# Retention and low-rank mixer on one core: load order of batch 1, place of batch 3's last loads, and first tiles of MLP1

## The chip, the cores and the metric

The kernel runs on one core of a Trainium2 chip. The metric is the device time of one execution in microseconds (us), given as the median of several runs. Engines are named as in the profile: PE (TensorE matmuls) with PEld (its weight loads), DVE (VectorE), ACT (ScalarE), POOL (GpSimd), SP (SyncE, which here issues nearly all DMAs; a row marked SPq is such an issue).

## What is computed

For each of 4 batches there are 768 tokens, 8 heads of 64 columns and a model width of 512. A retention layer gives x, and a mixer with a two-layer MLP follows:

```python
for t in range(S):                       # per head, gamma = 1 - 2^(-5-h)
    state = gamma * state + k[t] v[t]^T
    y[t] = q[t] @ state / sqrt(64)
x = y                                    # (4, 768, 512)
u = x + V^T (U^T x)                      # over tokens: U is 768x32, V is 32x768
out = u + relu(u @ w_ch1) @ w_ch2        # 512 -> 2048 -> 512
```

Inputs and output are fp32; the matmuls run in bf16.

## The kernel before

**Tiling.** A batch has six chunks of 128 tokens (c = 0 to 5). Retention is done chunk by chunk: kd and qd are k and q times powers of gamma (`ret_k`, `ret_q`, lines 251 and 256, both on POOL), vb is v cast to bf16 (`ret_v`, line 262, ACT). Kd and qd are transposed into qkT, for batch 1 on PE (`ret_T`, line 419, eight 128x128 transposes for a chunk) and for batches 2 and 3 by DMA (`ret_T_dma`, line 282, two DMA transposes on SP for a chunk). `ret_S` makes the masked scores a (line 441, DVE), `ret_O` the output x of a chunk (line 460, ACT). There are four buffers for qd and six for kd, and six for each of the loaded tiles k_n, q_n and v_n.

**The mixer.** `mix_P` makes P = U^T x. `mix_n` (lines 527 to 535) makes u for one chunk of tokens, j, adds x on DVE (line 531), casts it on ACT (line 533) and has it transposed into uT by a DMA on SP (line 535). Batches 2 and 3 do so for all six chunks, batch 1 for chunks 3 to 5; its chunks 0 to 2, the first half of uT, are made by PE in four pieces, one for each of the four 128-row blocks of the model width (`mix_u`), and evicted by ACT or DVE (`evict`, lines 120 and 124).

**The MLP.** `mlp1(b, m, hf)` is one tile: four matmuls of 384 columns (c = 0 to 3, the four blocks of uT) that sum into one PSUM bank, evicted with a relu into gT. There are 16 values of m and two halves hf of the tokens, 32 tiles in all, 128 matmuls. `mlp2` then takes, for each chunk of tokens, 16 matmuls of 512 columns, a DVE addition (line 576) and the DMA of the result (line 579).

**What sets the order.** The program is written out by hand, and every engine works in the order of the program. For each batch b the list of main slots (32 of MLP1, then 48 or more of MLP2) is woven with side work of batch b + 1: `put(side, i, f)` places f ahead of main slot i. While batch b runs its MLP, the retention and the mixer of batch b + 1 are done between its slots. All loads and DMA transposes share SP's queue, which issues in order. In the table of batch b = 0, all loads of batch 1 are placed at slot 14 (line 701), chunk by chunk as k, q, v (`load_chunk`, line 138; `load_one`, line 131; the issue itself is line 135). The first three loads are gated by a small ACT write (line 134), so that they do not start before slot 14. Loads of batch 3 stand in the table of b = 1, in `ret_side` at slots 31, 36, 41, 46, 68 and 72 (line 617), the u transposes of batch 2 at slots 62 to 67.

**MLP1's order.** For b of 1 and more, line 707 puts the first six tiles of the first half of the tokens first, then the six of the second half, and then alternates. Two DMA-transposed halves are so needed at different times. In batch 0 the first tiles go through `mlp1_two`, which takes two tiles at a time: blocks 0 and 1 of both, and then blocks 2 and 3 of both.

Of the kernel before, what the change touches and what calls it, by code (L numbers as in the profile page):

```python
# [47 lines left out]
def kernel(  # L48
# [14 lines left out]
    NCK = S // P  # L63
# [36 lines left out]
    def set_banks(main, mix=None):  # L100

        for who, banks in (("main", main), ("mix", mix)):
            use[who] = banks and sorted(banks, key=lambda i: taken.get(i, 0))
            n_use[who] = 0

    def mm_bank(who="main"):
        if use[who] is None:
            who = "main"
        b = use[who][n_use[who] % len(use[who])]
        n_use[who] += 1  # L110
        taken[b] = n_bank[0]
        return bank(b)

    def matmul(o, l, r, cols, **kw):
        nc.tensor.matmul(o, l, r, **kw)  # L115
        bal.mm(cols)

    def evict(o, i, cols, relu=False, dve_rate=1.0):
        if bal.pick(cols, dve_rate) == "A":
            nc.scalar.activation(o, i, AF.Relu if relu else AF.Copy)  # L120
        elif relu:
            nc.vector.tensor_relu(o, i)
        else:
            nc.vector.tensor_copy(out=o, in_=i)  # L124


    staged = {}
# [3 lines left out]
    def load_one(t, b, c, src, nm):  # L131
        n = rin.tile([P, H, D], fp32, tag=nm, name=f"{nm}_{b}_{c}")
        if (b, c) == gate:
            nc.scalar.activation(n[:, 0, :1], lsc, AF.Copy)
        nc.sync.dma_start(out=n, in_=src[b, :, ts(c, P), :].rearrange("h p d -> p h d"))  # L135
        t[nm, c] = n

    def load_chunk(b, c):
        t = {}
        for src, nm in ((k, "k_n"), (q, "q_n"), (v, "v_n")):  # L140
            load_one(t, b, c, src, nm)
        staged[b, c] = (t["q_n", c], t["k_n", c], t["v_n", c])

    NG = P // RK
    Vs = wts.tile([RK, S], bf16)
# [5 lines left out]
    def load_w1(lo, w):  # L151
        nc.gpsimd.dma_start(
            out=w1b[:, :, ds(lo, w)],
            in_=moe_w_ch1[:, ds(lo, w)].rearrange("(c p) m -> p c m", p=P))

    def load_w2(s):
        nc.gpsimd.dma_start(
            out=w2b[:, ds(4 * s, 4)],
            in_=moe_w_ch2[ts(s, 512)].rearrange("(j p) c -> p j c", p=P))
# [9 lines left out]
    for what in ("q0", "kA", "q1", "k2", "k3", "vA", "q2", "k4", "v2", "k5", "v3", "v4", "v5"):  # L169
        src, i = {"q": q, "k": k, "v": v}[what[0]], what[1]  # L170
# [75 lines left out]
    st_p = {}  # L246

    def ret_k(b, c, eng):
        q_n, k_n, v_n = staged.pop((b, c))
        kd = rmid.tile([P, H, D], bf16, tag="kd", name=f"kd_{b}_{c}", bufs=6)  # L250
        eng.tensor_tensor(kd, k_n, Gk[:, c].unsqueeze(2).to_broadcast([P, H, D]), op=ALU.mult)  # L251
        rc[b, c] = dict(kd=kd, q_n=q_n, v_n=v_n)
# [7 lines left out]
    def ret_v(b, c):  # L260
        vb = rmid.tile([P, H, D], bf16, tag="vb", name=f"vb_{b}_{c}", bufs=6)
        nc.scalar.activation(vb, rc[b, c]["v_n"], AF.Copy)  # L262
        bal.book("A", 0.63)
        rc[b, c]["vb"] = vb
# [4 lines left out]
    def ret_in(b, c):  # L269
        ret_k(b, c, nc.gpsimd)  # L270
        ret_q(b, c, nc.gpsimd)
        if b == 1 and c in EARLY:
            load_chunk(b + 1, c - EARLY[0])

    def by_dma(b):
        return b >= 2
# [148 lines left out]
    def ret_S(b, cs):  # L425

        for c, bks in zip(cs, ((SA, SB), (OB, TP if by_dma(b) else 2))):
            r = rc[b, c]
            r["s"] = [bank(i) for i in bks]
            for p in range(NP):  # L430
                for e in (0, 1):
                    matmul(r["s"][e][:, ts(p, P)], r["kT"][ds(D * e, D), p],
                           r["qT"][ds(D * e, D), p], 80, start=True, stop=True)
        for c in cs:
            rc[b, c]["a"] = rmid.tile([P, 2, NP, P], bf16, tag="a", name=f"a_{b}_{c}", bufs=5)
            for e in (0, 1):
                ret_mask(b, c, e)
# [109 lines left out]
    def mlp1_two(b, ms, hf):  # L547
        if b not in gTs:
            gTs[b] = gtp.tile([P, NM, S], bf16, tag="gT", name=f"gT_{b}")
        g = [mm_bank()[:, :HS] for _ in ms]  # L550
        for cs in ((0, 1), (2, 3)):
            for m, o in zip(ms, g):
                for c in cs:
                    matmul(o, w1b[:, c, ts(m, P)], uTs[b][:, c, ts(hf, HS)], HS, start=(c == 0),
                           stop=(c == NCB - 1))
        for m, o in zip(ms, g):
            evict(gTs[b][:, m, ts(hf, HS)], o, HS, relu=True)
# [23 lines left out]
    def mlp1_slots(b, first=0):  # L581
        return [lambda m=m, hf=hf: mlp1(b, m, hf) for m in range(first, NM) for hf in (0, 1)]

    def mlp2_slots(b, of=8):

        cols = {(B - 1, NCK - 1): ((0, DM // 2), (DM // 2, DM // 4), (3 * DM // 4, DM // 4))}
        return [lambda j=j, i=i: mlp2(b, j, i, 12 if (b, j) in cols else of,
                                      cols.get((b, j), ((0, DM),)))
                for j in range(NCK) for i in range(12 if (b, j) in cols else of)]

    def weave(main, side):

        for i, f in enumerate(main):
            for g in side.pop(i, []):
                g()
            f()
        for i in sorted(side):
            for g in side[i]:
                g()

    def put(side, i, f):
        side.setdefault(int(i), []).append(f)

    def ret_side(b, at, lead, S_at, O_at, side):


        for c in range(NCK):
            put(side, max(0, at[c] - lead), lambda c=c: ret_in(b, c))
            put(side, O_at[c] - 3, lambda c=c: ret_v(b, c))
        for cs in S_at:  # L610
            put(side, S_at[cs], lambda cs=cs: ret_S(b, cs))
        for f, when in ((ret_T, at), (ret_O, O_at)):
            for c in range(NCK):
                put(side, when[c], lambda c=c, f=f: f(b, c))
        if by_dma(b) and b + 1 < B:
            for c in range(NCK):
                put(side, (31, 36, 41, 46, 68, 72)[c], lambda c=c: load_chunk(b + 1, c))
        return side

    def mix_side(b, i, side):  # L620
        put(side, i + 2, lambda: mix_P(b))
        js = [j for j in range(NCK) if by_token(b, j)]
        for n, j in enumerate(js):
            put(side, i + 5 + n, lambda j=j: mix_n(b, j))
        if b == 1:
            for c in range(NCB):
                put(side, i + 5 + len(js) + c, lambda c=c: mix_u(b, 0, c))
        return side
# [56 lines left out]
    for b in range(B):  # L685
        nxt = b + 1 < B
        slots = mlp1_slots(b)
        n1 = len(slots)
        side = {}
        set_banks([0, 1, 2, SA, SB, OB])  # L690
        if b == 0:
            taken.update({i: n for n, i in enumerate((1, 2, 0, OB, SA, SB, TP))})
            set_banks([1, 2, 0, OB, SA, SB, TP])
            slots[:4] = [lambda: mlp1_two(0, (0, 1), 0), lambda: None,
                         lambda: mlp1_two(0, (0, 1), 1), lambda: None]
            for i, s in ((1, 2), (2, 3)):
                put(side, i, lambda s=s: load_w1(512 * s, 512))
            for s in range(4):
                put(side, 4 + s, lambda s=s: load_w2(s))
            for c in range(NCK):  # L700
                put(side, 14, lambda c=c: load_chunk(1, c))
            at, lead, mix_at = [n1 + 7 + 5 * c for c in range(NCK)], 4, n1 + 38
            S_at = {(0, 1): n1 + 14, (2, 3): n1 + 24, (4,): n1 + 30, (5,): n1 + 35}
            O_at = [n1 + i for i in (19, 22, 29, 32, 35, 38)]
        if b:

            slots = slots[:12:2] + slots[1:12:2] + slots[12:]
        if b and nxt:
            set_banks([0, 1, 2])
            at, lead, mix_at = [10 + 4 * c for c in range(NCK)], 5, n1 + 25  # L710
            S_at = {(0, 1): 27, (2, 3): 37, (4, 5): 47}
            O_at = [32, 35, 43, 46, 53, 56]
        if nxt:
            ret_side(b + 1, at, lead, S_at, O_at, side)
            put(side, n1, lambda: set_banks([0, 1], [2]))
            put(side, mix_at, lambda: use.update(mix=[2, SA, SB]))
            mix_side(b + 1, mix_at, side)
        if b == 1:
            for c, i in ((3, 0), (4, 7), (5, 15)):
                put(side, i, lambda c=c: load_chunk(2, c))  # L720
        weave(slots + mlp2_slots(b), side)


# [28 lines left out]
```

## Time and profile before

| what | value |
|---|---|
| median of 3 runs | 228.08 us (227.82 to 229.71) |
| the profiled execution | 228.57 us, of which the span of the profile is 226.80 us |
| granted TensorE clock | 1.00 |
| DMA over the span | 34.85 MB, mean 154 GB/s |
| start of MLP1 of batch 0, 1, 2, 3 | 27.43, 81.88, 131.92, 181.95 us from the span's start |

Rows of the profile give the start in us from the span's start, the length, the engine, the line of the kernel, the operation, output and inputs, and the number of merged instructions. In square brackets stands how long the engine sat idle ahead of the row, and what ended that. A matmul's end is modelled, so waits of PE are better read from the distance of two starts. In views of waits the numbers are the total in us, the count and the longest.

### The profile page before, as it was taken

To read this page: it belongs to the slowest core of one execution; us is meant where nothing else is said; L and a number is where in the kernel's file an instruction comes from. 1 tells how busy PE (TensorE), PEld (TensorE's weight loads), DVE (VectorE), ACT (ScalarE), POOL (GpSimd) and SP (SyncE) were. 2 spreads that over 40 slices of the span, in tenths; PEclk is the share of its full clock that TensorE was granted. 3 is DMA by queue.
4 is the path that set the end of the run, shared out by engine and by line. 5 is a ranking of instruction groups with operands and counts; after the bars stand their busy time and mean duration, and the time that the engine had idled before them with its cause. 6 is when DMAs were issued, how large, how long until landed. Compare 5 with 4: busy or idle time off the path is not lost.

```text
span 226.8 us, 4286 instructions
## 1 busy us (share of the span) xinstructions
PE 220.1 (97%) x1735; PEld 124.6 (55%) x1735; DVE 85.2 (38%) x162; ACT 112.3 (50%) x221; POOL 58.2 (26%) x65
## 2 busy tenths in 40 slices
PE   7998999999999999999999998999999999999994
PEld 2566666655556456656554455656554456654454
DVE  8498630004677430034673610035674410001221
ACT  3377667760355277767133546767223457760000
POOL 6856900036473512421046301130000000000000
DMA  6998999999999969999699969965211570001212
GB/s 174 244 263 174 175 205 200 198 196 230 197 249 240 230 181 209 190 180 101 133 219 235 263 105 225 215 95 95 72 46 48 139 142 0 0 3 46 83 56 94
DMA packets 100244, 34.85 MB, mean 154 GB/s; under 512 B 87136, under 2 KB 97280, under 8 KB 100224
## 3 DMA queue, kind: packets, MB, share of 16 engines
q1 hardware_dynamic: 94640, 30.29, 64.4%
q0 software_dynamic: 5584, 4.29, 12.6%
q8 instruction: 13, 0.21, 0.4%
q14 instruction: 7, 0.06, 0.1%
HBM read 27.46 MB, written 6.29 MB: 149 GB/s over the span
## 4 chain that ended last, share of the span: by engine, by line
PE 83%; DMA 6%; DVE 5%; SPq 2%; POOL 1%; ACT 1%; issue 1%; POOLq 0%; ACTq 0%
PE bk L115 82%; DMA k_n<-in_k_dram 3%; DMA q_n<-in_q_dram 2%; DVE a L346 2%; SPq L135 2%; DMA uT<-x 1%; POOL qd L256 1%; ACT st L293 1%; DVE qd L305 1%; PE bk L419 1%; POOL kd L251 0%; DVE kT L295 0%; DVE res L576 0%; DVE vb L295 0%; ACT kT L293 0%
## 5 line engine op out<-in xcount | busy, mean ns | idle before, releaser
L115 PE MATMUL bk<-w2b,gT 128*128 128x512 bf16 (+2 forms) x416 | 92.0, 363 | 0.0
L115 PE MATMUL bk<-uT,w1b 128*128 128x384 bf16 x512 | 84.7, 326 | 0.9 <-DMA uT<-x 0.8
L120 ACT ACTIVATE gT<-bk 128x384 bf16<-128x384 f32 x124 | 60.9, 491 | 32.9 <-PE bk L115 32.9
L115 PEld LDWEIGHTS <-w1b 128*128 128x128 bf16 x512 | 49.8, 98 | 34.6 <-issue 1.6
L115 PEld LDWEIGHTS <-gT 128*128 128x128 bf16 x416 | 37.9, 98 | 37.7 <-issue 0.8
L251 POOL TENSOR_TENSOR kd<-k_n,Gk 128x512 bf16<-128x512 f32 x18 | 18.8, 1043 | 72.1 <-DMA k_n<-in_k_dram 52.8
L441 DVE TENSOR_TENSOR a<-bk,mask 128x512 bf16<-128x512 f32 x36 | 22.4, 683 | 38.6 <-PE bk L115 38.4
L576 DVE TENSOR_TENSOR res<-bk,res 128x512 f32<-128x512 f32 (+2 forms) x17 | 10.6, 626 | 44.9 <-PE bk L115 44.9
L460 ACT ACTIVATE x<-bk 128x512 bf16<-128x512 f32 x18 | 10.7, 595 | 23.7 <-PE bk L115 23.7
L256 POOL TENSOR_TENSOR qd<-q_n,Gq 128x512 bf16<-128x512 f32 x18 | 18.8, 1043 | 11.4 <-DMA qkT<-qd 8.1
L479 DVE TENSOR_TENSOR state<-bk,bmask 128x512 bf16<-128x512 f32 x15 | 10.4, 691 | 10.7 <-PE bk L115 10.7
L531 DVE TENSOR_TENSOR res<-bk,x 128x512 f32<-128x512 f32 x15 | 9.7, 685 | 8.0 <-PE bk L115 8.0
L533 ACT ACTIVATE x<-res 128x512 bf16<-128x512 f32 x15 | 9.3, 630 | 6.8 <-DVE res L531 6.5
L115 PEld LDWEIGHTS <-qkT 64*128 64x128 bf16 (+1 forms) x204 | 8.4, 95 | 7.1 <-issue 3.2
L115 PE MATMUL bk<-idle 128*128 128x512 bf16 x29 | 10.4, 499 | 1.2 <-DVE idle L180 1.2
L262 ACT ACTIVATE vb<-v_n 128x512 bf16<-128x512 f32 x18 | 10.8, 622 | 0.8 <-DMA v_n<-in_v_dram 0.8
L124 DVE COPY qkT<-bk 128x1024 bf16<-128x1024 bf16 x3 | 2.1, 691 | 24.3 <-PE bk L419 24.3
L115 PE MATMUL bk<-vb,a 128*128 128x64 bf16 (+1 forms) x208 | 10.1, 193 | 0.0
L115 PE MATMUL bk<-P_sb,Vb 128*128 128x512 bf16 x24 | 9.1, 380 | 0.0
L120 ACT ACTIVATE qkT<-bk 128x1024 bf16<-128x1024 bf16 x3 | 3.1, 1024 | 11.8 <-PE bk L419 11.8
L115 PEld LDWEIGHTS <-a 128*128 128x128 bf16 (+1 forms) x208 | 8.5, 97 | 0.7
L115 PE MATMUL bk<-vb,kd 128*128 128x128 bf16 (+1 forms) x88 | 8.2, 219 | 0.2 <-ACT st L293 0.2
(85 smaller groups left out, 135.7 us busy)
## 6 DMA issues: line engine op xcount, KB each, us to landing
out_dram<-res SPq DMA_DIRECT2D x23, 256.0 KB, 2.4
k_n<-in_k_dram SPq DMA_DIRECT2D x22, 256.0 KB, 4.8
v_n<-in_v_dram SPq DMA_DIRECT2D x22, 256.0 KB, 4.9
q_n<-in_q_dram SPq DMA_DIRECT2D x18, 256.0 KB, 4.8
w2b<-in_moe_w_ch_dram POOLq DMA_DIRECT2D x4, 512.0 KB, 15.9
in<-in_q_dram SPq DMA_DIRECT2D x3, 512.0 KB, 6.3
w1b<-in_moe_w_ch_dram POOLq DMA_DIRECT2D x3, 512.0 KB, 8.9
in<-in_k_dram SPq DMA_DIRECT2D x1, 512.0 KB, 5.9
```

The costliest lines, as they stand in the source:

```text
L115: nc.tensor.matmul(o, l, r, **kw)
L120: nc.scalar.activation(o, i, AF.Relu if relu else AF.Copy)
L135: nc.sync.dma_start(out=n, in_=src[b, :, ts(c, P), :].rearrange("h p d -> p h d"))
L251: eng.tensor_tensor(kd, k_n, Gk[:, c].unsqueeze(2).to_broadcast([P, H, D]), op=ALU.mult)
L256: eng.tensor_tensor(qd, rc[b, c]["q_n"], Gq[:, c].unsqueeze(2).to_broadcast([P, H, D]), op=ALU.mult)
L262: nc.scalar.activation(vb, rc[b, c]["v_n"], AF.Copy)
L441: nc.vector.tensor_tensor(r["a"][:, e], r["s"][e].rearrange("p (n t) -> p n t", n=NP), mask4, op=ALU.mult)
L460: nc.scalar.activation(xs[b][:, c], o, AF.Copy)
L479: nc.vector.tensor_tensor(sb, ps.rearrange("p (n t) -> p n t", n=NP), bmask4, op=ALU.mult)
L531: nc.vector.tensor_tensor(u, h, xs[b][:, j], op=ALU.add)
L533: nc.scalar.activation(xs[b][:, j], u, AF.Copy)
L576: nc.vector.tensor_tensor(o, chp.pop((b, j)), o if by_token(b, j) else xs[b][:, j, ds(lo, w)], op=ALU.add)
```

## The change

Three places change; the arithmetic stays as it is.

1. Batch 1's loads, still all at slot 14 of batch 0, are issued with k and q ahead of v: k0 q0 k1 q1 k2 q2 v0 k3 q3 v1 k4 q4 v2 v3 k5 q5 v4 v5, in place of k0 q0 v0 k1 q1 v1 and so on.
2. For b of 1 and more MLP1 begins with eight tiles of the first half in place of six, and then eight of the second. In batch 1 the first two of them go through `mlp1_two`.
3. Batch 3's loads of chunks 4 and 5 move from slots 68 and 72 of batch 1's table to slots 0 and 7 of batch 2's, that is, from ahead of one each of batch 1's last two output DMAs to behind both. The transposes of u of batch 2 stand ahead of them in SP's queue in both kernels.

```diff
-    def load_chunk(b, c):
-        t = {}
-        for src, nm in ((k, "k_n"), (q, "q_n"), (v, "v_n")):
-            load_one(t, b, c, src, nm)
-        staged[b, c] = (t["q_n", c], t["k_n", c], t["v_n", c])
+    def load_chunk(b, c, kinds="kqv"):
+        t = staged.setdefault((b, c), {})
+        for nm in kinds:
+            load_one(t, b, c, {"k": k, "q": q, "v": v}[nm], nm + "_n")
...
-        q_n, k_n, v_n = staged.pop((b, c))
+        q_n, k_n, v_n = (staged[b, c][nm + "_n", c] for nm in "qkv")
...
-            for c in range(NCK):
-                put(side, (31, 36, 41, 46, 68, 72)[c], lambda c=c: load_chunk(b + 1, c))
+            for c, i in enumerate((31, 36, 41, 46)):
+                put(side, i, lambda c=c: load_chunk(b + 1, c))
...
-            for c in range(NCK):
-                put(side, 14, lambda c=c: load_chunk(1, c))
+            for c, nm in ((0, "kq"), (1, "kq"), (2, "kq"), (0, "v"), (3, "kq"), (1, "v"), (4, "kq"),
+                          (2, "v"), (3, "v"), (5, "kq"), (4, "v"), (5, "v")):
+                put(side, 14, lambda c=c, nm=nm: load_chunk(1, c, nm))
...
-            slots = slots[:12:2] + slots[1:12:2] + slots[12:]
+            slots = slots[:16:2] + slots[1:16:2] + slots[16:]
+        if b == 1:
+            slots[:2] = [lambda: mlp1_two(1, (0, 1), 0), lambda: None]
...
-        if b == 1:
-            for c, i in ((3, 0), (4, 7), (5, 15)):
-                put(side, i, lambda c=c: load_chunk(2, c))
+        if b in (1, 2):
+            for c, i in ((3, 0), (4, 7), (5, 15)) if b == 1 else ((4, 0), (5, 7)):
+                put(side, i, lambda c=c: load_chunk(b + 1, c))
```

On the engines this leaves the counts of instructions as they were, but for one relu eviction of batch 1 (of one of its first two MLP1 tiles), which goes from ACT to DVE.

## The prediction

> **What bounds the kernel.** First the page: which engine is full, and of what the chain that ended last is made.
>
> ```profile
> PE 220.1 (97%) x1735; PEld 124.6 (55%) x1735; DVE 85.2 (38%) x162; ACT 112.3 (50%) x221; POOL 58.2 (26%) x65
> PE 83%; DMA 6%; DVE 5%; SPq 2%; POOL 1%; ACT 1%; issue 1%; POOLq 0%; ACTq 0%
> ```
>
> PE is the bound. The change adds and removes no matmul, so all that it can win is time in which PE stands still. Next the chain in order of time, which shows where something else than PE stood on the path after the start:
>
> ```profile
> 53.24 5.77 DMA k_n<-in_k_dram
> 61.27 0.62 PE bk L419 x8
> 81.42 0.69 DVE res L576
> 82.12 0.54 DVE uT L124
> 82.69 50.56 PE bk L115 x380
> 133.26 3.39 DMA uT<-x
> 136.78 86.94 PE bk L115 x604
> ```
>
> There are three such places: at 61.27 (a load of k, then POOL), at 82.69 (the last piece of uT of batch 1), at 136.78 (the last DMA transpose of u of batch 2). To size them I take the timeline of PE and compare starts.
>
> ```profile
> 59.61 1.46 PE L115 MATMUL bk<-w2b,gT 128*128 128x512 bf16 x6
> 61.27 0.40 PE L419 MATMUL bk<-ident,qd 128*128 128x128 bf16 x4 [0.20 <-POOL qd L256]
> 81.88 18.03 PE L115 MATMUL bk<-uT,w1b 128*128 128x384 bf16 x108
> 99.85 0.62 PE L115 MATMUL bk<-qkT 64*128 64x128 bf16 x16
> 126.31 5.78 PE L115 MATMUL bk<-w2b,gT 128*128 128x512 bf16 x26
> 131.92 4.06 PE L115 MATMUL bk<-uT,w1b 128*128 128x384 bf16 x24
> 136.78 3.41 PE L115 MATMUL bk<-uT,w1b 128*128 128x384 bf16 x20 [0.80 <-DMA uT<-x]
> 139.71 10.89 PE L115 MATMUL bk<-uT,w1b 128*128 128x384 bf16 x66
> 150.53 0.62 PE L115 MATMUL bk<-qkT 64*128 64x128 bf16 x16
> 181.95 20.96 PE L115 MATMUL bk<-uT,w1b 128*128 128x384 bf16 x128
> 202.75 20.96 PE L115 MATMUL bk<-w2b,gT 128*128 128x512 bf16 x128
> ```
>
> A matmul of 384 columns takes (202.75 - 181.95) / 128 = 0.1625 us, one of 512 takes (131.92 - 126.31) / 26 = 0.216 us. So six of 512 from 59.61 end at 60.91, and PE came to 61.27: **0.36 us** lost. From 81.88, 108 of 384 columns need 17.55 us, that is 99.43, and the row of qkT starts at 99.85. Of these 0.42 us about 0.09 belong to that switch itself (139.71 and 66 x 0.1625 make 150.44, and its like starts at 150.53): **0.33 us** lost. From 131.92, 24 of them end at 135.82, and PE went on at 136.78: **0.96 us** lost. Together 1.65 us, 0.7% of the span. Each part of the change lies at one of these places, and the first 28 us, where PE also waits, are not touched.
>
> **Part 1: k and q ahead of v.** The 18 loads are as large as before and stand at the same 18 places in SP's queue, so I leave the pace of the places as it was and only move names.
>
> ```profile
> 49.63 1.41 SPq L135 DMA_DIRECT2D k_n<-in_k_dram  x1
> 51.09 0.91 SPq L135 DMA_DIRECT2D q_n<-in_q_dram  x1
> 52.09 1.05 SPq L135 DMA_DIRECT2D v_n<-in_v_dram  x1
> v_n<-in_v_dram SPq DMA_DIRECT2D x22, 256.0 KB, 4.9
> L262 ACT ACTIVATE vb<-v_n 128x512 bf16<-128x512 f32 x18 | 10.8, 622 | 0.8 <-DMA v_n<-in_v_dram 0.8
> 59.16 0.40 PE L115 MATMUL bk<-vb,a 128*128 128x64 bf16 x8
> 61.95 0.40 PE L115 MATMUL bk<-vb,a 128*128 128x64 bf16 x8
> 139.04 1.04 POOL L251 TENSOR_TENSOR kd<-k_n,Gk 128x512 bf16<-128x512 f32 x1 [10.74 <-PE bk L115]
> ```
>
> The first three rows are places 7 to 9; the fourth gives the median time to landing, the last (of chunk 4 of batch 3) what one kd or qd takes on POOL. Chunk 3's k and q go from places 10 and 11 to 8 and 9: k is issued at 51.09 in place of 53.24 (the first row of the chain above), q at 52.09. They land by 57.0 at the median; kd and qd of chunk 3 on POOL (1.04 us each) are then done by about 58.1, and PE wants them at 60.91. The wait of 0.36 us goes. Chunks 4 and 5 gain places too (k4 from 13 to 11, k5 from 16 to 15). The price is paid by v: v0 goes from place 3 to place 7, and lands at about 49.63 + 4.9 = 54.5. Its cast on ACT (0.62 us) is done by 55.3, and PE first reads it at 59.16. V1, at place 10, was seen to land 5.77 us after 53.24, at 59.01; after the cast it is there by 60.1, and PE reads it at 61.95 less 0.36. So v costs nothing: its cover is 3.9 us for v0 and 1.5 us for v1; beyond that each us late would be one of PE. On ACT, which is in order, the next work behind the cast of v0 is the eviction of chunk 2's qkT, which PE makes later than that. Term: -0.36.
>
> **Part 2: eight tiles, two of them paired.** In batch 1 the pair runs blocks 0 and 1 of both tiles, four matmuls or 0.65 us, before it needs block 2. The DVE copy of the last block ends at 82.12 + 0.54 = 82.66, and in the new order block 3 is first read at 81.88 + 5 x 0.1625 = 82.69. The second tile's bank is emptied by the DVE addition that ends at 82.11, and it is wanted at 82.20. Both fit by a hair (0.03 and 0.09 us); term between -0.33 and -0.25, I take -0.33. The eviction that goes to DVE finds it idle.
>
> In batch 2 eight tiles are 32 matmuls, 5.20 us, in place of 3.90 before the second half of uT is wanted: 131.92 + 5.20 = 137.12, and the last transpose lands at 133.26 + 3.39 = 136.65. The 0.96 us go. But when this wait goes and PE comes 0.36 + 0.33 = 0.69 us earlier, what is late next? The first half of uT:
>
> ```profile
> 131.83 3.77 PEld L115 LDWEIGHTS <-w1b 128*128 128x128 bf16 x24 [0.24 <-DMA uT<-x]
> 79.56 5.00 SPq L535 DMA_TRANSPOSE uT<-x  x3
> SPq L535 <- ACT x L533: 1.5, 1, 1.5
> 126.08 2.54 SPq L535 DMA_TRANSPOSE uT<-x  x2
> 129.33 6.02 SPq L535 DMA_TRANSPOSE uT<-x  x4
> ```
>
> The third transpose landed just before 131.83, when PE's first weights of batch 2 were loaded: with PE at 131.23 there is no slack left. From the transposes of 79.56 on SP's issues follow each other closely, so these transposes come earlier only as far as SP does, and SP's last long wait for PE's work was the transpose at 79.56, which waited for x on ACT. X comes 0.36 us earlier there (part 1's gain); the 0.33 us of batch 1's start lie behind it and do not reach SP. So the transposes move by between 0 (if transfers and not issues set the pace) and 0.69 us; I take 0.36, since the wait row is at that place. PE then starts batch 2 at 131.56, and 0.33 of the 0.69 us are given back. Term of part 2 and this wait: -0.33 - 0.96 + 0.33 = -0.96. In batch 3, where the same waits could come, rows show none before (128 matmuls from 181.95 at full pace), and eight tiles add slack.
>
> **Part 3: two chunks of loads moved.** The transposes of u of batch 2 already stand ahead of both chunks, so they gain nothing. K of chunk 4 lands some 2 us later, since two outputs go first.
>
> ```profile
> 146.52 1.04 POOL L256 TENSOR_TENSOR qd<-q_n,Gq 128x512 bf16<-128x512 f32 x1 [6.44 <-DMA qkT<-qd]
> 142.64 1.22 SPq L282 DMA_TRANSPOSE qkT<-qd  x1
> DMA to landing us min/median/max: 2.4/2.4/2.5
> ```
>
> Kd of chunk 4 then runs near 141 and not at 139.04 (part 1's last row), but POOL waits for a free qd buffer until 146.52 anyway, and chunk 5's loads land before. The queue holds the same eight DMAs ahead of 142.64, so the transposes of qkT start there as before. The last row is of the three transposes issued from 145.28 to 147.9; the one that completes chunk 1 goes out at 146.54 and so lands near 149.0. PE's scores want it some 0.25 us after 150.53 - 1.3: 149.5. It fits. Term 0. Nothing waits for the outputs that now go first, so it is no gain; as a loss I bound it by one load's issue, about 1 us, less the slack of 0.85 us worked out under (d): 0.15 us.
>
> **Sum.** -0.36 - 0.96 + 0 = -1.32 us: 228.57 for the profiled execution becomes 227.25. That execution was 0.49 us above the median of 228.08, so against the median I say 226.8 us. Bounds of the terms: -1.65 (all waits go) and -0.96 (the transposes do not move).
>
> **Rivals.** (a) *The transposes do not move at all*: 228.08 - 0.96 = 227.1. For it: loads in a row are issued about 1 us apart (part 1's rows), so transfers may set the pace. Against it: the idle time of SP before 79.56. (b) *All move with PE*: 228.08 - 1.65 = 226.4. Against it: SP's queue has no pause behind 79.56 for the 0.33 us to enter by. (c) *The 0.96 us were no steady wait.* Two transposes of u took longer to land than their like:
>
> ```profile
> q8 instruction: 1, 0.02, 8.7%
> DMA to landing us min/median/max: 4.0/4.0/4.0
> ```
>
> These are the DMA view of 132.5 to 133.5, with one fetch of instructions, and the transpose issued at 131.95 (the like in part 3: 2.4). Had the last one landed 2.4 us after 133.26, at 135.66, PE at 135.82 would not have waited, and eight tiles would win nothing. Then about 228.08 - 0.36 = 227.7 remains. Against it: a fetch belongs to a place in an engine's program, and the programs keep their lengths up to there, so it should fall near the same tile each time. Runtime: NRT & Kernel Launch, in Instruction fetch mechanics, of the Trainium skill, says that crossing such a boundary is mostly hidden, which would speak for (c); here the trace has 1.6 us more beside the fetch.
>
> ```profile
> 38.50 5.46 SPq L135 DMA_DIRECT2D v_n<-in_v_dram  x1
> 139.96 1.58 SPq L135 DMA_DIRECT2D v_n<-in_v_dram  x1
> ```
>
> (d) *Slower*: the six loads and two outputs hold up the transposes of qkT of batch 3. From 0.85 us of slip (149.0 less 0.36 against 149.5) PE waits for its scores, and from 2.2 us the kernel is slower than before. One issue of SP like the one of 5.46 us at 38.50 would give 228.08 - 1.32 + 5.46 - 0.85 = 231.4. Against it: of the eight issues from 135.4 to 142.5 the longest took 1.58 us. (e) *Part 3's loads come late*: k of chunk 4, 2 us later, costs those 2 us, 228.08 - 1.32 + 2 = 228.8. Against it: POOL waits past 146 for a buffer in any case, so k would have to land 5 us later still. DMA: Bandwidth & Descriptors, in Rules for kernel authors, of the Trainium skill, speaks for (e): issue a DMA early, wait for it late; the trace does not bear it out for this load, whose kd has over 5 us to spare.
>
> **How the numbers follow.** Forecast 0.50, (a) 0.20, (b) 0.13, (c) 0.11, (d) 0.04, (e) 0.02. The range 225.9 to 228.1 holds all but (d), (e) and some scatter: below, (b) less 0.5, since the three runs lie up to 0.26 below their median and more above it; above, no gain at all. A measurement of this kernel tells about 1% from no change, and 1% is 2.28 us. All waits together are 1.65, so faster by over 1% needs (b) or the forecast with scatter beside: 0.13. Slower by over 1% is (d): 0.04. The rest, 0.83, is within 1%.
>
> **What would show it.** Right: in the timeline of PE no gap before the transposes of chunk 3 near 61, none in the first pair of batch 1, none after tile eight of batch 2, and a small one, about 0.3 us, at the first tile of batch 2, ended by a transpose of u. Wrong: a wait of PE for vb, a gap ahead of the scores of batch 3 (150.53 before), or the last transpose of u landing later than 5.2 us after the start of MLP1.

## The result, and the profile after

| | before | after |
|---|---|---|
| median | 228.69 us (227.82 to 229.71, 13 runs) | 227.76 us (227.05 to 228.81, 13 runs) |
| profiled execution | 228.57 us, span 226.8 us | 228.08 us, span 226.3 us |

The ratio of the two is 0.9955 [0.9935, 0.9975]: about 1.0 us faster, between 0.6 and 1.5 us. The prediction gave a chance of 0.83 to a difference within 1%. The forecast was -1.32 us; the two profiled executions stand 0.49 us apart.

First from the page of the changed kernel what the chain that ended last is made of.

```profile
PE 84%; SPq 6%; DMA 4%; DVE 2%; ACT 2%; issue 1%; POOL 0%
```

PE's share was 83% before, that of DMA 6%. Next the chain in order of time, cut to its places behind the start where something else than PE stood on the path.

```profile
125.34 2.43 ACT x L532 x4
129.67 2.46 DMA uT<-x
132.17 42.14 PE bk L115 x339
174.90 0.69 DVE res L530
175.63 47.60 PE bk L115 x283
```

The three places of before (61.27, 82.69, 136.78) are gone. Two others stand there: the third DMA transpose of u of batch 2, which releases PE at 132.17, and a DVE addition at 174.90. The timeline of PE gives their sizes.

```profile
27.55 1.22 PE L115 MATMUL bk<-uT,w1b 128*128 128x384 bf16 x6
59.74 1.46 PE L115 MATMUL bk<-w2b,gT 128*128 128x512 bf16 x6
61.03 0.39 PE L418 MATMUL bk<-ident,qd 128*128 128x128 bf16 x4
81.63 17.71 PE L115 MATMUL bk<-uT,w1b 128*128 128x384 bf16 x108
99.28 0.62 PE L115 MATMUL bk<-qkT 64*128 64x128 bf16 x16
125.74 5.78 PE L115 MATMUL bk<-w2b,gT 128*128 128x512 bf16 x26
132.17 17.72 PE L115 MATMUL bk<-uT,w1b 128*128 128x384 bf16 x108 [0.65 <-DMA uT<-x]
174.99 0.59 PE L115 MATMUL bk<-w2b,gT 128*128 128x512 bf16 x2
175.63 0.38 PE L115 MATMUL bk<-P_sb,Vb 128*128 128x512 bf16 x1
```

Read by starts, as in the prediction: six matmuls of 0.216 us from 59.74 end at 61.03, where the transposes of chunk 3 start, so no wait is left there (-0.36). The 108 matmuls from 81.63 and the step to qkT take 17.65 us, which is 108 x 0.1625 + 0.09: no wait in batch 1's first pair (-0.33). The 108 from 132.17 are one unbroken row, so none behind tile eight (-0.96). New is the wait at the first tile of batch 2: 26 x 0.216 from 125.74 end at 131.36, and PE came at 132.17 (+0.81). Two matmuls from 174.99 end at 175.42, and the next came at 175.63 (+0.21). MLP1 of batch 0 started 0.12 us later (27.55 against 27.43), in a part that the change does not touch. The sum, -0.36 - 0.33 - 0.96 + 0.81 + 0.21 + 0.12 = -0.51, is the difference of the spans.

So all three waits went as meant, and half of what they gave came back at one place. Why there? Here are SP's issues of the changed kernel up to the six transposes of u of batch 2 (before, they are the prediction's rows at 126.08 and 129.33), and two rows of its view of DMA between 132.5 and 133.5 us.

```profile
110.69 0.59 SPq L135 DMA_DIRECT2D k_n<-in_k_dram  x1
...
124.76 1.56 SPq L578 DMA_DIRECT2D out_dram<-res  x2
126.41 2.54 SPq L534 DMA_TRANSPOSE uT<-x  x2
129.67 6.06 SPq L534 DMA_TRANSPOSE uT<-x  x4
```

```profile
q8 instruction: 1, 0.02, 8.9%
uT<-x SPq DMA_TRANSPOSE x1, 4.0
```

The transposes did not come earlier with PE; here they came 0.33 us later (126.41 against 126.08). And the fetch of instructions is at nearly the same time as before, again with a transpose beside it that takes 4.0 us to land.

### The profile page after: what moved, and what is told of

The parts are those of the page before. It is cut to its first block, busy times and chain, and to the rows that moved or that the text cites. A ratio compares the mean times of both kernels' runs of the same rounds, so it can differ in the third digit from the quotient of the medians.

```text
span 226.3 us, 4287 instructions
## 1 busy us (share of the span) xinstructions
PE 220.0 (97%) x1735; PEld 124.7 (55%) x1735; DVE 85.4 (38%) x163; ACT 112.2 (50%) x220; POOL 58.2 (26%) x65
## 4 chain that ended last, share of the span: by engine, by line
PE 84%; SPq 6%; DMA 4%; DVE 2%; ACT 2%; issue 1%; POOL 0%
PE bk L115 82%; DMA k_n<-in_k_dram 3%; SPq L135 3%; SPq L165 2%; PE bk L418 1%; DVE res L530 1%; DMA uT<-x 1%; ACT x L532 1%; DVE res L575 1%; SPq L534 1%; POOL kd L299 0%; ACT st L292 0%; ACT kT L292 0%; SPq L578 0%; PE bk L311 0%
## 5 line engine op out<-in xcount | busy, mean ns | idle before, releaser
L440 DVE TENSOR_TENSOR a<-bk,mask 128x512 bf16<-128x512 f32 x36 | 22.4, 683 | 36.9 <-PE bk L115 36.7
L345 DVE TENSOR_TENSOR a<-bk,mask 128x512 bf16<-128x512 f32 x12 | 7.7, 686 | 1.7 <-PE bk L115 1.7
```

What stands on the lines that cost most here:

```text
L345: nc.vector.tensor_tensor(r0["a", c][:, e], r0["s", c][e].rearrange("p (n t) -> p n t", n=NP), mask0[:, c].unsqueeze(1).to_broadcast([P, N ...
L440: nc.vector.tensor_tensor(r["a"][:, e], r["s"][e].rearrange("p (n t) -> p n t", n=NP), mask4, op=ALU.mult)
```

## The experiments

My theory after the result: PE's gain of 0.7 us ahead of batch 2 cannot be kept, because the transposes of u stand in SP's queue behind batch 3's loads of chunks 0 to 3, and the pace of those loads, not x, sets when they start. The rivals: they do follow x, as the prediction had it, and this execution was an accident; the wait of 0.96 us came from the fetch and not from the order of the tiles; part 3 costs something.

### The parts alone

**e1_kq_first**: before, with part 1 alone.

```diff
-            for c in range(NCK):
-                put(side, 14, lambda c=c: load_chunk(1, c))
+            for c, nm in ((0, "kq"), (1, "kq"), (2, "kq"), (0, "v"), (3, "kq"), (1, "v"), (4, "kq"),
+                          (2, "v"), (3, "v"), (5, "kq"), (4, "v"), (5, "v")):
+                put(side, 14, lambda c=c, nm=nm: load_chunk(1, c, nm))
```

> Part 1 alone (k and q of batch 1 ahead of v). Both theories: the 0.36 us wait of PE ahead of chunk 3's transposes near 61 is gone. Forecast (the transposes of u of batch 2 follow x on ACT): they land 0.36 us earlier too, PE starts batch 2 near 131.56, the wait of 0.96 us behind tile six stays, time -0.36 us. Rival (a) (SP's queue sets when they land): the first transposes of u still land at about 131.8 or later, PE waits 0.36 us at the first tile of batch 2, time 0.

Measured: ratio 1.0012 [0.9989, 1.0035]. SP's issues, then PE:

```profile
79.19 4.71 SPq L534 DMA_TRANSPOSE uT<-x  x3
129.38 5.93 SPq L534 DMA_TRANSPOSE uT<-x  x4
```

```profile
60.92 0.39 PE L418 MATMUL bk<-ident,qd 128*128 128x128 bf16 x4
81.52 18.03 PE L115 MATMUL bk<-uT,w1b 128*128 128x384 bf16 x108
131.84 4.07 PE L115 MATMUL bk<-uT,w1b 128*128 128x384 bf16 x24
```

The transposes of chunk 3 start at 60.92, with no wait, and batch 1's MLP starts at 81.52 in place of 81.88. In batch 1 the transposes of u even followed x by 0.37 us (79.19 against 79.56). But in batch 2 the four last ones were issued at 129.38 (before: 129.33), and PE started MLP1 at 131.84 (before: 131.92). Of the gain of 0.36 us, 0.28 us are given back at batch 2's transposes: in this execution the step "transposes follow x" holds for one batch and is lost on the way to the next.

**e2_pair** (before, with `slots[:2] = [lambda: mlp1_two(1, (0, 1), 0), lambda: None]` for b = 1 alone), **e3_eight** (before, with `slots[:16:2] + slots[1:16:2] + slots[16:]` alone) and **e4_late45** (before, with part 3 alone):

> The pair of tiles in batch 1 alone. Both theories: no step over 0.17 us in the first six matmuls of batch 1's MLP1 (0.33 us lost there before), and the 0.33 us come back as a wait at the first tile of batch 2, since no transpose of u hangs on it: time 0. If PE's gains were kept: -0.33 us.

> Eight tiles of the first half first, alone. Forecast and rival (a): the wait of 0.96 us behind tile six of batch 2 is gone, nothing else moves, time -0.96 us. Rival (c) (the wait is no steady one): about 0.

> Batch 3's chunks 4 and 5 loaded behind the last two outputs of batch 1, alone. Forecast and rival (a): time 0 within 0.15 us, POOL's kd of chunk 4 about 2 us later than 139.04 and its qd still near 146.5. Rival (e) (loads come late): +2 us.

Measured: 1.0019 [0.9994, 1.0045], 0.9974 [0.9948, 0.9999] and 1.0005 [0.9979, 1.0031]. From e2_pair, then e3_eight:

```profile
82.28 17.71 PE L115 MATMUL bk<-uT,w1b 128*128 128x384 bf16 x108
132.57 4.07 PE L115 MATMUL bk<-uT,w1b 128*128 128x384 bf16 x24 [0.41 <-DMA uT<-x]
```

```profile
81.44 18.03 PE L115 MATMUL bk<-uT,w1b 128*128 128x384 bf16 x108
125.86 5.78 PE L115 MATMUL bk<-w2b,gT 128*128 128x512 bf16 x25
131.48 9.26 PE L115 MATMUL bk<-uT,w1b 128*128 128x384 bf16 x56
```

The pair takes its 0.32 us out of batch 1 (17.71 us in place of 18.03), and by its ratio it wins nothing. A wait at batch 2's first tile is there too, but this execution does not show that the 0.32 us went there: it had lost 0.78 us near 61, so PE came no earlier than before, and the four last transposes were issued from 130.10 on. The eight tiles take out the wait behind tile six whole and are the only part that wins by itself, though barely clear of no change (0.9999). Their profiled execution, 227.18 us, was the fastest of twelve with a median of 228.41: it happened to have no wait near 61, without part 1, and so began batch 1's MLP at 81.44. Part 3 alone does nothing that shows. Part 1, the pair and the eight tiles alone come to +0.0012, +0.0019 and -0.0026 from a ratio of 1: only the last counts, and the whole change with its -0.0045 is not far from it.

### The loads in front of the transposes

**e5_late345**: the changed kernel, with batch 3's chunk 3 loaded behind the transposes of u of batch 2 as well. **e6_before_late3**: the same move of chunk 3 in the kernel before (slot 46 to slot 68).

```diff
-            for c, i in enumerate((31, 36, 41, 46)):
+            for c, i in enumerate((31, 36, 41)):
...
-            for c, i in ((3, 0), (4, 7), (5, 15)) if b == 1 else ((4, 0), (5, 7)):
+            for c, i in ((3, 0), (4, 7), (5, 15)) if b == 1 else ((3, 0), (4, 0), (5, 7)):
```

> The changed kernel, and batch 3's chunk 3 loaded behind the transposes of u of batch 2 as well (three loads fewer ahead of them in SP's queue, about 3.3 us at 1.1 us each). If SP's queue sets when the transposes of u land (rival a): the third lands near 129, PE does not wait at the first tile of batch 2 (0.81 us in the changed kernel's profile), time about -1.6 us against the kernel before, -0.6 us against the changed one. If they hung on x: no move, time as the changed kernel. If the loads now come too late: PE waits for qkT ahead of batch 3's scores near 149.

> The kernel before, with batch 3's chunk 3 loaded behind the transposes of u of batch 2 and nothing else changed. If SP's queue sets their landing: all six land about 3 us earlier, so the wait of 0.96 us behind tile six is gone without eight tiles: -0.96 us. If the wait belongs to tile six and not to the queue: 0.

Measured: 0.9996 [0.9970, 1.0021] and 1.0019 [0.9995, 1.0043]. SP, then PE, of e5_late345:

```profile
124.05 2.50 SPq L534 DMA_TRANSPOSE uT<-x  x2
...
143.80 1.93 SPq L281 DMA_TRANSPOSE qkT<-qd  x1
...
148.40 1.27 SPq L281 DMA_TRANSPOSE qkT<-kd  x1
```

```profile
131.32 17.71 PE L115 MATMUL bk<-uT,w1b 128*128 128x384 bf16 x108
148.97 0.40 PE L115 MATMUL bk<-qkT 64*128 64x128 bf16 x8
150.91 0.40 PE L115 MATMUL bk<-qkT 64*128 64x128 bf16 x8 [1.54 <-DMA qkT<-kd]
```

With three loads fewer in front, the first transposes of u go out at 124.05 in place of 126.41, and PE starts batch 2 at 131.32 with no idle time ahead of it: the loads are what pinned them. Rows of ACT's cast of x, which the transposes read, show the same; they are of before, of the changed kernel and of e9_spread (below), where the three loads are also out of the way.

```profile
124.00 1.35 ACT L533 ACTIVATE x<-res 128x512 bf16<-128x512 f32 x2 [1.71 <-DVE res L531]
123.43 1.35 ACT L532 ACTIVATE x<-res 128x512 bf16<-128x512 f32 x2 [1.72 <-DVE res L530]
123.30 1.35 ACT L532 ACTIVATE x<-res 128x512 bf16<-128x512 f32 x2 [1.72 <-DVE res L530]
```

In the changed kernel the cast came 0.57 us earlier than before and the transposes 0.33 us later, 2.98 us behind the cast's start. In all five kernels with the three loads moved (e5, e6, e8, e9 and e12) they go out 0.65 us behind it, and in the nine others 1.4 to 3.0 us: x sets them only once these loads are gone.

Yet the time is not better than before. Nine loads now stand in one row behind the transposes of u, the first transpose of qkT goes out at 143.80 (before: 142.64) and the one that completes chunk 1 at 148.40 (before: 146.54), and PE waits for its scores. Sixteen matmuls of qkT take 0.55 us (e9_spread below: 148.87 to 149.42), so eight from 148.97 end at 149.25, and the others start at 150.91: 1.66 us, more than was won. This is rival (d) of the prediction, made true by three loads more. In e6_before_late3 the wait behind tile six was gone as well (108 matmuls in one row from 132.17), and the same wait for scores stood at 151.68, ended by the same transpose of kd.

**e9_spread**: the changed kernel, with chunk 3 as in e5_late345, but chunks 4 and 5 later, behind the transposes of qkT of batch 3's first two and first three chunks. **e10_only45**: that place for chunks 4 and 5 alone, chunk 3 as in the changed kernel. **e11_after_again**: the changed kernel itself once more. The edit of e9_spread (in e10_only45 the second list is `((4, 15), (5, 19))` and the first line is as in the changed kernel):

```diff
-            for c, i in enumerate((31, 36, 41, 46)):
+            for c, i in enumerate((31, 36, 41)):
...
-            for c, i in ((3, 0), (4, 7), (5, 15)) if b == 1 else ((4, 0), (5, 7)):
+            for c, i in ((3, 0), (4, 7), (5, 15)) if b == 1 else ((3, 0), (4, 15), (5, 19)):
```

> The changed kernel, with chunk 3 of batch 3 loaded behind the transposes of u of batch 2 (as in e5_late345), and chunks 4 and 5 not in a row behind it but later, behind the transposes of qkT of the first two chunks of batch 3. My theory (the 0.7 us of PE won before batch 2 are given back because loads in front of the transposes of u pin them, and in e5_late345 they were given back 18 us later since the same queue then held up the transposes of qkT): the transposes of u land 3 us before PE wants them as in e5_late345, the transposes of qkT of chunks 0 and 1 land before 149.0 since six loads fewer stand ahead of them, and PE waits at neither place; the span is 0.8 us under that of the changed kernel's page (226.3), so 225.5, and the ratio to before near 0.992. Rival: the queue's total is what counts, and every load put off comes back as a wait somewhere; then PE waits 0.5 us or more for chunk 4's or chunk 5's qkT or for vb in the second half of batch 2, and the ratio is 0.996 to 1.000.

> The changed kernel with chunks 4 and 5 of batch 3 loaded behind the transposes of qkT of the first two chunks of batch 3; chunk 3 stays ahead of the transposes of u. My theory: the wait at batch 2's first tile stays (0.3 to 0.8 us, as in the changed kernel), the transposes of qkT land 3 us earlier than in the changed kernel and nobody needs them earlier, so the ratio is that of the changed kernel, 0.995 to 0.997. Rival (loads put off come back as waits): 0.5 us or more of new waits of PE behind 150, ratio 0.998 to 1.000.

> The changed kernel again, for a comparison on the same chip as e9_spread and e10_only45. Ratio 0.9955 as found before; one wait of 0.3 to 0.8 us at batch 2's first tile, none behind tile eight.

Measured: e9_spread 227.17 us (227.09 to 227.43), ratio to before 0.9917 [0.9887, 0.9948], span 225.4; e10_only45 0.9955 [0.9934, 0.9976]; e11_after_again 228.23 us (227.31 to 229.86), 0.9966 [0.9937, 0.9996]. SP, then PE, of e9_spread; then one row of PE of e11_after_again:

```profile
123.95 2.54 SPq L534 DMA_TRANSPOSE uT<-x  x2
...
136.50 1.55 SPq L281 DMA_TRANSPOSE qkT<-qd  x1
...
140.72 1.27 SPq L281 DMA_TRANSPOSE qkT<-kd  x1
142.03 0.58 SPq L135 DMA_DIRECT2D k_n<-in_k_dram  x1
```

```profile
125.61 5.78 PE L115 MATMUL bk<-w2b,gT 128*128 128x512 bf16 x26
131.22 17.71 PE L115 MATMUL bk<-uT,w1b 128*128 128x384 bf16 x108
148.87 0.62 PE L115 MATMUL bk<-qkT 64*128 64x128 bf16 x16
149.42 3.42 PE L115 MATMUL bk<-uT,w1b 128*128 128x384 bf16 x20
```

```profile
131.92 17.72 PE L115 MATMUL bk<-uT,w1b 128*128 128x384 bf16 x108 [0.43 <-DMA uT<-x]
```

E9_spread came out as the theory had it: no wait of PE at batch 2's first tile, none at the scores, and a span of 225.4 us (expected 225.5). E10_only45 shows that the later place of chunks 4 and 5 does nothing by itself; the wait at batch 2's first tile stands as in the changed kernel (PE idle up to 132.21). The changed kernel again had that wait, 0.59 us this time (26 matmuls of 512 columns from 125.71 end at 131.33). So this wait is steady in kind and varies in size: 0.81, 0.59 and, in e10_only45, 1.05 us.

**e12_before_spread**: the kernel before, with nothing but the loads of e9_spread.

> The kernel before, with only batch 3's loads moved as in e9_spread (chunk 3 behind the transposes of u of batch 2, chunks 4 and 5 behind the transposes of qkT of batch 3's first two chunks); part 1 and part 2 are not in it. My theory (what pins the transposes of u is the row of loads in front of them): the transposes of u land some 3 us earlier against PE, so the wait behind tile six of batch 2 goes without eight tiles, and no wait comes at the scores of batch 3; what stays are the waits near 61 (0.36 us) and in batch 1's first pair (0.33 us). Span 226.8 - 0.96 = 225.8, ratio near 0.996, and the 0.7 us by which e9_spread is shorter are parts 1 and the pair, kept there. Rival: the eight tiles are what takes the 0.96 us away; then a wait of 0.3 us or more stays behind tile six of batch 2 and the ratio is 0.998 or more.

Measured: 227.89 us (227.36 to 229.68), ratio 0.9943 [0.9919, 0.9967].

```profile
61.59 0.40 PE L419 MATMUL bk<-ident,qd 128*128 128x128 bf16 x4 [0.64 <-POOL qd L256]
82.20 18.04 PE L115 MATMUL bk<-uT,w1b 128*128 128x384 bf16 x108
132.25 17.71 PE L115 MATMUL bk<-uT,w1b 128*128 128x384 bf16 x108
```

Batch 2's 108 matmuls are one unbroken row with six tiles first: the moved loads take the wait behind tile six away without part 2. The waits of parts 1 and 2 stand (0.80 us at 61.59 in this execution, 0.33 us in batch 1's first pair). So these moves of three chunks of loads are worth about as much as the whole change, and with them in place the change adds about 0.6 us more by the two ratios (0.9943 to 0.9917; their intervals overlap).

### The fetch beside the transposes

**e7_fetch_moved**: the kernel before, with each idle matmul of 512 columns at the start (its result is not used) made as four of 128, so that PE's program is longer and its fetches fall elsewhere. **e8_late345_fetch** does the same to e5_late345.

```diff
-            matmul(w, idle[:, :P], idle, DM, start=True, stop=True)
+            for i in range(DM // P):
+                matmul(w[:, ts(i, P)], idle[:, :P], idle[:, :P], P, start=True, stop=True)
```

> The kernel before, with each idle matmul of 512 columns at the start made of four of 128 columns: the same columns, 174 PE instructions more ahead of MLP1, and nothing else changed. If the fetch of instructions at 132.90 belongs to PE's program and holds up the transposes: the fetches move to other places by about 174 PE instructions (near 118 and 138), the transposes of u issued behind 131 land 2.4 to 2.5 us after issue as their like do, the wait behind tile six is gone or under 0.2 us, time about -0.9 us. If the late landings have another cause: the wait of 0.96 us stays, time 0.

> e5 and e7 together. If both causes are right, neither adds to the other in batch 2 (e5 already leaves no wait there): time as e5, -1.6 us against the kernel before. If the fetch costs elsewhere too: below e5.

Measured: 1.0065 [1.0037, 1.0093] and 1.0110 [1.0070, 1.0149]. Both lose time at the start, where the edit is (MLP1 of batch 0 begins at 29.82 in e7_fetch_moved and at 28.98 in e8_late345_fetch, before at 27.43). Why they do stays open, so their times do not price the fetch; the rows show what it does. Of e7_fetch_moved the view of DMA from 131.8 to 138.3 us, which has no row of q8 now, and PE:

```profile
uT<-x SPq DMA_TRANSPOSE x4, 2.5
```

```profile
134.37 7.95 PE L115 MATMUL bk<-uT,w1b 128*128 128x384 bf16 x47 [0.26 <-DMA uT<-x]
```

With the fetch elsewhere the four last transposes land 2.5 us after their issue, in place of 4.0 and 3.4 for the last two. 47 matmuls are 7.64 us and the modelled end of the last adds 0.16, so 0.15 us of wait are left in this row in place of 0.96; another 0.43 us stand ahead of it, at batch 2's first tile (PE was ready at 133.94). In e8_late345_fetch the waits for batch 3's scores stayed (1.55 us at 153.61, ended by a transpose of kd), so the fetch is not their cause. But there the fetch now falls beside transposes of qkT of batch 2. Two rows of its view of DMA from 106 to 108 us, and PE:

```profile
q8 instruction: 1, 0.02, 4.7%
qkT<-kd SPq DMA_TRANSPOSE x1, 4.5
109.58 0.40 PE L115 MATMUL bk<-qkT 64*128 64x128 bf16 x8 [1.06 <-DMA qkT<-kd]
```

That transpose landed after 4.5 us, and PE waited 1.17 us for it (eight matmuls from 108.13 end at 108.41). So a moved fetch costs at its new place, if a transpose that PE waits for is in flight there.

## Why the prediction was right, and where it was not

**Part 1, -0.36: right, with a size that is one execution's.** The wait near 61 went, in the changed kernel and alone, and no profile with part 1 has it. Without part 1 it was 0.36 us in the profile of before, but 0 in e3_eight and e7_fetch_moved, 0.17 in e4_late45, and 0.73 to 0.80 in e2_pair, e6_before_late3 and e12_before_spread. The margin was smaller than was worked out: qd of chunk 3 was forecast for 58.1 and ran from 59.12 to 60.16, as POOL's row of the changed kernel shows, with PE wanting it at 61.03.

```profile
59.12 1.04 POOL L255 TENSOR_TENSOR qd<-q_n,Gq 128x512 bf16<-128x512 f32 x1 [1.08 <-DMA q_n<-in_q_dram]
```

PE did not wait for v, as said.

**The pair, -0.33, and the eight tiles, -0.96: right.** Each went at its place and alone. The wait behind tile six was steady: 0.96 in e1_kq_first, 1.17 in e2_pair and 0.70 in e4_late45.

**The wait that takes their place, +0.33: the step that failed.** The prediction named the place (batch 2's first tile) and the releaser (a transpose of u), and had the transposes follow x by 0.36 us. They did not: in e1_kq_first, where x of batch 1 came earlier and the transposes at 79.19 with it, those of batch 2 were issued at 129.38, as before. In the changed kernel's profile they did not even follow in batch 1: x was cast from 78.65 in place of 78.90, and the transposes went out at 79.90, right behind three outputs. The idle time of SP ahead of 79.56, on which the step rested, is some 50 us upstream, and between 110.69 and 126.41 SP's queue in the changed kernel holds only twelve loads and three outputs, one close behind the other. That they pin the transposes is shown: with three loads fewer they go out 2.4 us earlier, 0.65 us behind x (e5_late345, e9_spread). That was the mechanism of rival (a), which forecast all 0.69 us of give-back; 0.81, 0.59 and 1.05 were seen. By it the sum is -0.96, and -0.93 is the distance of the medians; e11_after_again, with 0.9966 or about -0.8, shows that so close a match is partly luck. The number 226.8 lies 0.96 below the median after of 227.76; 0.6 of that is that the kernel before ran at 228.69 beside it and not at 228.08, and the rest is this step. The range held in spite of the step, since it took in rival (a) as well.

**(c), the fetch: half right, and harmless to the forecast.** The late landing is the fetch's doing (e7_fetch_moved), as (c) said. It is no accident of one execution: the changed kernel has it at the same time, since the programs keep their lengths up to there, and the eight tiles win against it. The Trainium skill (Runtime: NRT & Kernel Launch, Instruction fetch mechanics) has such a crossing mostly hidden; that holds here for PE itself, whose 108 matmuls from 132.17 run on across it, but not for the transposes in flight, which land up to 1.6 us later.

**Part 3, 0: right.** E4_late45 gave 1.0005, and e10_only45 against e11_after_again 0.9955 against 0.9966. Its rivals (d) and (e) did not come. (d) came in e5_late345, three loads beyond the change. The prediction's working had chunk 1 complete with a transpose issued at 146.54 - 0.36 = 146.18, and PE 1.3 us early, with a slack of 0.85 us. In e5_late345 that transpose went out at 148.40, 2.22 us later, and PE came 1.56 us early (148.97 against 150.53), 0.26 us more: 2.22 + 0.26 - 0.85 = 1.63 us, and 1.66 were lost. Its size was right too.

**Not foreseen:** 0.21 us at 175.63, behind a DVE addition that the chain shows at 174.90. It stood in e9_spread, e10_only45 and e11_after_again as well, at a neighbouring place in e2_pair, e5_late345 and e8_late345_fetch, and in e6_before_late3, which has nothing of parts 1 and 2; not in e1_kq_first, e3_eight, e4_late45, e7_fetch_moved or e12_before_spread. Its cause stays open.

## What to carry to other kernels

When several waits lie one behind the other, follow the queue that feeds the later ones before adding up the gains: what a faster engine wins is kept only as far as that queue has slack, and a queue that waited for the engine 50 us earlier may be bound by its own loads by then. Sharing one in-order queue, loads that nobody needs soon belong behind the transfers that somebody waits for, and spread between them: here three loads moved out of the way and six moved later were worth as much as the three parts of the change (0.9943 and 0.9955), while nine in one row only moved the wait 18 us on. DMA: Bandwidth & Descriptors of the Trainium skill (Rules for kernel authors: issue early, wait late) is thus to be read for each queue as a whole: here the loads issued early were the ones that cost.

## What the hardware showed beyond that

A transpose of SBUF data that was in flight beside a fetch of 16 KB of instructions (13 fetches moved 0.21 MB) landed after 4.0 us in place of 2.4 to 2.5, in both kernels. It was 3.9 to 4.1 us at the longest in all twelve kernels whose fetch fell among the transposes of u of batch 2; once the fetch was elsewhere, the last four landed after 2.4 to 2.5 us.

With SP's queue full of loads of 256 KB, one DMA went out in about 1.05 us: twelve loads and three outputs took 15.7 us in the changed kernel (110.69 to 126.41) and 15.6 before (110.44 to 126.08), though PE was 0.6 us ahead in the former. In the six other kernels that keep all twelve loads and the fetch in place, e1 to e4, e10 and e11, the same stretch took 15.5 to 16.1 us. It began anywhere from 109.2 to 110.8, so the first transposes went out from 124.98 (e3_eight) to 126.87 (e2_pair). A few tenths of a us in the place of a transpose of one profile are therefore scatter.
